# Moving the low-bits step of the w1 and w2 conversion from VectorE to ScalarE in a pooled-attention and gated-MLP kernel

## The chip, the cores and the metric

The kernel runs on one core of one Trainium2 chip. The core has five engines that each work through their own queue in order: TensorE (PE in the profile, with its weight loads as PEld), VectorE (DVE), ScalarE (ACT), GpSimd (POOL) and SyncE (SP), which here only issues DMAs. The metric is the device time of one execution in microseconds. Before the change the median of three runs is 786.11 us (785.08 to 788.28).

## The reference

Attention over 8 batches, 8 heads, 576 tokens and 64 dimensions, whose keys and values are averaged over groups of 8 tokens, and then an MLP over the 4608 tokens:

```python
k_p = k.reshape(B, H, 72, 8, D).mean(axis=3)
v_p = v.reshape(B, H, 72, 8, D).mean(axis=3)
attn = softmax(q @ k_p.T / sqrt(D))
x = (attn @ v_p) as (4608, 512)
a = x @ w1                  # w1, w2: 512 x 1024
b = x @ w2
h = a * b @ w3              # w3: 1024 x 1024
out = h @ w_out             # w_out: 1024 x 512, result float32
```

q, k and v are float32. The four weights are float64, so each of their values is two 32-bit words in memory, and the kernel itself makes float32 values of them.

## The kernel before, in words

**Weights.** The kernel multiplies w3 by w_out once, to a matrix W (`w_mm`, line 624), so that the MLP is (a * b) @ W. A float32 operand is split into a high part and a low part (`split`, lines 152 and 153: ScalarE copies to the reduced type, VectorE or GpSimd subtracts), and three matmuls stand for one product (`PASSES`).

**From float64 to float32.** A weight tile arrives as a raw cell: 128 partitions of 1024 int32 words, that is 512 float64 values. Three steps make float32 bits of it. `high` (line 135, ScalarE, Prelu) turns the high word into z. `low` (line 140, VectorE) shifts the low word right by 29, which leaves its top three bits in r. `conv_b` (line 148, VectorE) joins them as (z << 3) | r. `conv_a` is `high` and `low` together. For w1 and w2, `w12_conv` calls `conv_a` for one cell out of 16 (eight column groups j, two matrices w), `w12_conv2` calls `conv_b`, and `w12_split` splits the result into hl cells: its copy is on ScalarE, its subtraction on GpSimd, except for the three cells of LO_DVE. The results r lie in five buffers that are used in turn, z in three. The conversion of w3 and w_out uses the same helpers, in `w_block` and `w_conv`.

**Main loop.** The tokens go in 12 chunks m of 384. For each chunk and each of eight column groups j, TensorE computes a = x w1 (12 matmuls, line 563, tile a), b = x w2 (12 matmuls, line 563, tile b), and adds the product g = a * b times W to three accumulators (9 matmuls, line 598). ScalarE copies a (line 573), VectorE multiplies (line 583), ScalarE makes g's high part gh (line 584), VectorE its low part gl (line 589). The attention of chunk n is woven into the MLP of chunk n-1: scores (line 404), their minimum (line 420) and exponential (line 422, 425 and 426, or for some token tiles of the first two chunks line 430 on ScalarE alone), the scaling by the sum (lines 439 to 442), the remainder columns R (ScalarE line 451, VectorE line 453), the transposes of E and R on TensorE (lines 464 and 474) and their copies (lines 520 to 527), the product with v (lines 537 to 540) and its split into xT (lines 548 and 549). The pooled keys km are summed by VectorE (line 319) or GpSimd (lines 362 to 364) and turned by TensorE (line 328).

**What sets the order.** The order is written by hand. `at(kind, k, ...)` puts each piece at a step k; pieces are sorted by whole step, then loads, vector work (P), main matmuls (M) and attention matmuls (A), then by the fraction of the step. All engines run what they get in that order. With M0 = 36 the step at which the main loop begins, the conversion of cell i = 2j + w stands at step M0 - 6 + 1.25 i, its `conv_b` one step later and its split four steps later. So the sixteen conversions lie between the last products for W and the first chunk of the MLP.

PSUM tiles of the attention (`att`) rotate through three buffers: a transpose of R at line 474 can start only when the engines have read the score tile that held its buffer before.

Of the kernel before, what the change touches and what calls it, by code (L numbers as in the profile page):

```python
# [8 lines left out]
F32 = mybir.dt.float32  # L9
F32R = mybir.dt.float32r  # L10
I32 = mybir.dt.int32
AF = mybir.ActivationFunctionType
ALU = mybir.AluOpType
AX = mybir.AxisListType
# [4 lines left out]
def kernel(  # L19
# [14 lines left out]
    nc = tc.nc  # L34
# [41 lines left out]
        out=msk,  # L76
        in_=ident.rearrange("p (a two e) -> p two a e", two=2, e=2 * KR),
# [10 lines left out]
    def f(ap):  # L88
        return ap.bitcast(F32)
# [4 lines left out]
    def raw_cell(i):  # L94
        return cp.tile([P, 1024], I32, tag=f"c{i}", name="raw")

# [4 lines left out]
    def W_cell(s, i, dt):  # L101
        return cp.tile([P, DM], dt, tag=f"W{s}_{i}", name="Wc")

    raw, w3t, wo, w12, W = {}, {}, {}, {}, {}
    FREED = (8, 0, 9, 1, 10, 2, 11, 3, 12, 4, 13, 5, 14, 6, 15, 7)
    w1r, w2r, w3r, wor = (w.bitcast(I32) for w in (moe_w1, moe_w2, moe_w3, moe_w_out))
    stage = {}
# [22 lines left out]
    def high(c, z):  # L130

        w = c.rearrange("p (c t) -> p c t", t=2)
        nc.scalar.activation(out=z, in_=w[:, :, 1].bitcast(F32), func=AF.Prelu, scale=2.0 ** -112, alpha=2.0 ** 32)

    def low(c, r):

        w = c.rearrange("p (c t) -> p c t", t=2)
        nc.vector.tensor_scalar(out=r, in0=w[:, :, 0], scalar1=29, scalar2=None, op0=ALU.logical_shift_right)  # L140

    def conv_a(c, r, z):
        high(c, z)
        low(c, r)

    def conv_b(r, z):

        nc.vector.scalar_tensor_tensor(  # L148
            out=r, in0=z.bitcast(I32), scalar=3, in1=r, op0=ALU.logical_shift_left, op1=ALU.bitwise_or)

# [4 lines left out]
    def w_tiles(s):  # L155
        if s == 0:
            stage["wt"] = [t[:, i] for t, x in (
                (p1.tile([P, x, 512], I32, tag=tag, name="wt"), x)
                for tag, x in (("PTh", 3), ("PTx", 4))) for i in range(x)]
        if s < NJ:  # L160
            stage["wo", s] = stage["wt"][s % 4], f(stage["wt"][4 + s % 3])
        stage["w3", s] = W_cell(0, 4 + s % 4, I32), W_cell(1, 4 + s % 4, F32)

# [45 lines left out]
    def w_conv(s):  # L209
        w_tiles(s)  # L210
        conv_a(raw.pop(("w3", s)), *stage["w3", s])
# [9 lines left out]
    def w12_conv(j, w):  # L221
        i = 2 * j + w
        if i == 0:
            wb = [xp.tile([P, 3, 512], I32, tag=f"xT{x}", name="wb") for x in range(2)]
            spare = [osp.tile([P, 512], I32, tag="ob", name="wb") for _ in range(2)]
            stage["wb"] = [wb[0][:, x] for x in range(3)] + spare, [wb[1][:, x] for x in range(3)]
        r, z = stage["wb"]
        stage["w12", j, w] = r[i % 5], f(z[i % 3])
        conv_a(raw.pop(("w12", j, w)), *stage["w12", j, w])

    def w12_conv2(j, w):
        conv_b(*stage["w12", j, w])
# [144 lines left out]
    def prep_vr(b):  # L377
# [4 lines left out]

        nc.scalar.activation(out=f(hi), in_=f(hi), func=AF.Copy, scale=msk[:, 0:1])
        nc.scalar.activation(out=m, in_=m, func=AF.Copy, scale=msk[:, 1:2])
        stage["vrp", b] = f(hi), m
# [25 lines left out]
    def soft1(n, t, half):  # L411
# [9 lines left out]
        if (n, t) not in SOFT_ACT:  # L421
            nc.vector.tensor_tensor(  # L422
                out=E[:nt, hs], in0=sv,
                in1=mx[:nt, hs].unsqueeze(2).broadcast_to([nt, 4, KP]), op=ALU.subtract)
            nc.scalar.activation(out=E[:nt, hs], in_=E[:nt, hs], func=AF.Exp, scale=-1.0)  # L425
            nc.vector.reduce_sum(out=sm[:nt, hs], in_=E[:nt, hs], axis=AX.X)  # L426
            return
        for i in range(4):
            h = 4 * half + i
            nc.scalar.activation(  # L430
                out=E[:nt, h], in_=sv[:, i], func=AF.Exp, scale=-1.0, bias=mx[:nt, h:h + 1],
                accum_out=sm[:nt, h:h + 1])
# [290 lines left out]
    for j in range(NJ):  # L723
        for w in range(2):
            i = 2 * j + w
            at("L", K0 + 8.5 + i, load_w12, j, w)
            k = M0 - 6 + 1.25 * i
            at("P", k, w12_conv, j, w)
            at("P", k + 1, w12_conv2, j, w)
            at("P", k + 4, w12_split, j, w)  # L730
# [66 lines left out]
```

## Time and profile before

| | |
|---|---|
| median of three runs | 786.11 us (785.08 to 788.28) |
| profiled execution, its own time | 787.77 us |
| span of the profiled execution, first to last instruction | 785.9 us |
| granted TensorE clock, mean | 0.991 |
| busy: TensorE, weight loads, VectorE, ScalarE, GpSimd | 97%, 90%, 61%, 35%, 26% of the span |

How to read it: a group's row names line, engine, operation, the written and the read tile, the shape and the count; a duration is of the instruction itself, waiting for a port or an operand inside the instruction included. In a timeline row the first number is the start in us from the start of the span, the second the time it covers, and the bracket says how long the engine had been idle and who released it. In the answer for one source line, three numbers are the shortest, median and longest duration in ns.

### The profile page before, as it was taken

How to read it: one execution, taken by the hardware profiler on the slowest of the kernel's cores; microseconds unless marked ns; L12 is line 12 of the kernel's file. 1: busy time of each engine (PE TensorE's matmuls, PEld its weight loads, DVE VectorE, ACT ScalarE, POOL GpSimd, SP SyncE). 2: the span in 40 equal slices, each digit the busy share in tenths (PEclk: the TensorE clock that was granted, in tenths of full speed). 3: DMA queues.
4: the chain of work that ended last, by engine and by line, in shares of the span. 5: the costliest groups of instructions: out<-in, count | busy, mean ns of one | idle time of the engine just before them, and what ended most of it. 6: DMA issues, size and time to landing. Idle time of an engine off the chain costs nothing.

```text
span 785.9 us, 11514 instructions
## 1 busy us (share of the span) xinstructions
PE 759.7 (97%) x4146; PEld 703.7 (90%) x4146; DVE 479.2 (61%) x939; ACT 278.5 (35%) x694; POOL 201.1 (26%) x234
## 2 busy tenths in 40 slices
PE   8898888999999999999999999999999999999998
PEld 7677777899999998999999998999999998999997
DVE  6957988576475477476484586574574675662211
ACT  5566655332233233232233233332332333332211
POOL 2254564204307403005208202016125220000000
PEclk9999999999999999999999999999999999999999
DMA  9998970016326332036144223037144232120101
GB/s 328 292 209 200 282 152 10 1 61 129 66 79 134 71 98 55 16 86 140 32 129 93 77 81 71 15 101 140 41 122 94 75 75 47 47 55 1 40 1 41
DMA packets 123913, 74.43 MB, mean 95 GB/s; under 512 B 75600, under 2 KB 107600, under 8 KB 123856
## 3 DMA queue, kind: packets, MB, share of 16 engines
q1 hardware_dynamic: 123856, 73.69, 38.2%
q8 instruction: 33, 0.54, 0.3%
q14 instruction: 24, 0.20, 0.1%
HBM read 52.43 MB, written 9.44 MB: 79 GB/s over the span
## 4 chain that ended last, share of the span: by engine, by line
PE 74%; DVE 15%; ACT 3%; DMA 3%; issue 3%; SPq 1%; DVEq 0%
PE o L598 22%; PE a L563 21%; PE b L563 21%; PE att L404 3%; DMA st<-in_v_dram 2%; PE o L624 2%; DVE T L487 2%; DVE E L442 1%; DVE wb L148 1%; DVE wb L140 1%; PE att L538 1%; PE att L540 1%; PE att L539 1%; DVE mx L420 1%; PE att L537 1%
## 5 line engine op out<-in xcount | busy, mean ns | idle before, releaser
L563 PE MATMUL a<-xT,hl 128*128 128x384 f32 x1152 | 222.1, 341 | 0.0
L563 PE MATMUL b<-xT,hl 128*128 128x384 f32 x1152 | 220.8, 339 | 0.4 <-DVE Wc L153 0.4
L563 PEld LDWEIGHTS a<-xT,hl 128*128 128x128 f32 x1152 | 202.5, 189 | 4.5 <-POOL hl L153 0.2
L563 PEld LDWEIGHTS b<-xT,hl 128*128 128x128 f32 x1152 | 199.7, 188 | 0.8 <-DVE Wc L153 0.8
L598 PE MATMUL o<-Wc,gh 128*128 128x512 f32 x576 | 180.6, 395 | 0.0
L362 POOL TENSOR_TENSOR st<-st 72x512 f32<-72x512 f32 (+1 forms) x53 | 77.8, 1469 | 224.5 <-DMA st<-in_k_dram 172.1
L598 PEld LDWEIGHTS o<-Wc,gh 128*128 128x128 f32 x576 | 106.7, 188 | 17.0
L583 DVE TENSOR_TENSOR a<-b,a 128x384 f32<-128x384 f32 x96 | 52.8, 550 | 112.6 <-PE b L563 112.6
L598 PE MATMUL o<-Wc,gl 128*128 128x512 f32 x288 | 114.3, 397 | 3.1 <-DVE gl L589 3.1
L584 ACT CAST gh<-a 128x384 fp32r<-128x384 f32 x96 | 49.2, 513 | 154.8 <-DVE a L583 154.8
L573 ACT COPY a<-a 128x384 f32<-128x384 f32 x96 | 46.0, 479 | 109.8 <-PE a L563 88.0
L425 ACT ACTIVATE E<-E 128x288 f32<-128x288 f32 (+1 forms) x70 | 31.1, 445 | 123.4 <-DVE E L422 123.4
L589 DVE TENSOR_TENSOR gl<-a,gh 128x384 fp32r<-128x384 f32 x96 | 64.0, 667 | 13.0 <-ACT gh L584 13.0
L598 PEld LDWEIGHTS o<-Wc,gl 128*128 128x128 f32 x288 | 54.1, 188 | 16.9 <-DVE gl L589 4.4
L549 DVE TENSOR_TENSOR xT<-att,xT 128x384 fp32r<-128x384 f32 x48 | 26.5, 556 | 60.3 <-ACT xT L548 60.3
L375 POOL TENSOR_TENSOR vbd<-vm,vbd 64x256 fp32r<-64x256 f32 x16 | 12.1, 759 | 180.1 <-ACT vbd L374 179.5
L426 DVE TENSOR_REDUCE sm<-E 128x4 f32<-128x288 f32 (+1 forms) x70 | 31.6, 452 | 35.8 <-ACT E L425 35.8
L404 PE MATMUL att<-kbd,qT 128*128 128x144 f32 (+1 forms) x320 | 52.6, 288 | 0.2 <-ACT E L430 0.2
L404 PEld LDWEIGHTS att<-kbd,qT 128*128 128x128 f32 (+1 forms) x320 | 47.8, 180 | 4.3 <-ACT E L430 0.5
L153 DVE TENSOR_TENSOR PTx<-PTx,PTh 128x512 fp32r<-128x512 f32 (+1 forms) x33 | 24.7, 749 | 35.1 <-ACT PTh L152 31.7
L420 DVE TENSOR_REDUCE mx<-att 128x4 f32<-128x288 f32 (+1 forms) x80 | 35.3, 441 | 17.7 <-PE att L404 17.6
L363 POOL TENSOR_TENSOR st<-st 72x256 f32<-72x256 f32 (+1 forms) x53 | 44.4, 837 | 4.2
(91 smaller groups left out, 811.6 us busy)
## 6 DMA issues: line engine op xcount, KB each, us to landing
raw<-in_moe_w_dram SPq DMA_DIRECT2D x32, 512.0 KB
PTx<-T SPq DMA_DIRECT2D x120, 96.0 KB
st<-in_k_dram SPq DMA_DIRECT2D x32, 288.0 KB
out_dram<-ob SPq DMA_DIRECT2D x35, 256.0 KB
st<-in_v_dram SPq DMA_DIRECT2D x32, 256.0 KB
qs<-in_q_dram SPq DMA_DIRECT2D x128, 48.0 KB
raw<-in_moe_w_out_dram SPq DMA_DIRECT2D x8, 512.0 KB
st<-in_v_dram SPq DMA_DIRECT2D x64, 64.0 KB
```

What stands on the lines that cost most here:

```text
L362: nc.gpsimd.tensor_tensor(out=t[:, :, 0:4], in0=t[:, :, 0:4], in1=t[:, :, 4:8], op=ALU.add)
L363: nc.gpsimd.tensor_tensor(out=t[:, :, 0:2], in0=t[:, :, 0:2], in1=t[:, :, 2:4], op=ALU.add)
L404: nc.tensor.matmul(out=ps[:nt, 2 * KP * j:2 * KP * (j + 1)], lhsT=qT[n][:, pr, off:off + nt], rhs=kbd[b % 2][:, pr], start=True, stop=True,)
L420: nc.vector.tensor_reduce(out=mx[:nt, hs], in_=sv, axis=AX.X, op=ALU.min)
L425: nc.scalar.activation(out=E[:nt, hs], in_=E[:nt, hs], func=AF.Exp, scale=-1.0)
L426: nc.vector.reduce_sum(out=sm[:nt, hs], in_=E[:nt, hs], axis=AX.X)
L563: nc.tensor.matmul(out=o, lhsT=w12[j, w][sw][:, kt * P:(kt + 1) * P], rhs=x[sx][:, kt], start=(i == 0), stop=(i == 3 * NK - 1))
L573: nc.scalar.copy(out=a, in_=gt[m, j][:, :CH])
L583: nc.vector.tensor_tensor(out=g, in0=ps[:, :CH], in1=g, op=ALU.mult)
L584: nc.scalar.copy(out=gh, in_=g)
L589: nc.vector.tensor_tensor(out=gl, in0=g, in1=f(gh), op=ALU.subtract)
L598: nc.tensor.matmul(out=oacc[m][t], lhsT=(gh, gl)[sg][:, c], rhs=W[j][sw], start=(j == 0 and i == 0), stop=(j == NJ - 1 and i == 2))
```

## The change

`w12_conv` hands `conv_a` another function for the low bits, `low_act`. It reads the raw cell as uint16, four halves to a float64 value, and takes the second of them, the upper half of the low word. ScalarE computes half * 2^-13 + 2^-14 - 0.5, and the conversion to int32 at the write rounds to the nearest whole number, which is the half shifted right by 13: the same three bits as the low word shifted right by 29. VectorE's shift (line 140) is no longer issued for w1 and w2; for w3 and w_out it stays.

```diff
+U16 = mybir.dt.uint16
...
+    def low_act(c, r):
+
+        w = c.bitcast(U16).rearrange("p (c t) -> p c t", t=4)
+        nc.scalar.activation(out=r, in_=w[:, :, 1], func=AF.Copy, scale=2.0 ** -13, bias=2.0 ** -14 - 0.5)
+
-    def conv_a(c, r, z):
+    def conv_a(c, r, z, low=low):
         high(c, z)
         low(c, r)
...
-        conv_a(raw.pop(("w12", j, w)), *stage["w12", j, w])
+        conv_a(raw.pop(("w12", j, w)), *stage["w12", j, w], low=low_act)
```

## The prediction

> **What bounds the kernel now.** I read the page's first two parts, then the waits of TensorE between 65 and 160 us, then the timelines of VectorE, ScalarE, GpSimd and TensorE in that stretch, and the answers for the two source lines that are exchanged.
>
> ```profile
> PE 759.7 (97%) x4146; PEld 703.7 (90%) x4146; DVE 479.2 (61%) x939; ACT 278.5 (35%) x694; POOL 201.1 (26%) x234
> ...
> PE   8898888999999999999999999999999999999998
> ...
> DVE  6957988576475477476484586574574675662211
> ```
>
> A slice is 19.6 us. From the eighth slice on TensorE is at 9 almost to the end, so what is gained or lost before about 142 us moves all that follows, one for one. VectorE is fullest (7 to 9) in slices 4 to 7, which is where the sixteen conversions of w1 and w2 lie. TensorE's waits there, in order of their totals (us in total, times, longest):
>
> ```profile
> PE att L474 <- ACT E L430: 4.8, 2, 3.9
> PE att L474 <- DVE E L422: 2.0, 1, 2.0
> PE att L328 <- DVE km L319: 1.6, 1, 1.6
> ...
> PE b L563 <- DVE Wc L153: 0.4, 1, 0.4
> ```
>
> The four rows are 8.8 us together: this is the purse from which a gain can come. All of them end on chains through VectorE and ScalarE.
>
> ```profile
> L140 DVE TENSOR_SCALAR wb<-raw x16: 410/550/1528, 73.0 to 129.8; 128x512 int32<-128x512 int32 x16
> ...
> L140 DVE TENSOR_SCALAR wb<-raw 128x512 int32<-128x512 int32 x16 | 12.8, 802 | 0.0
> ...
> L135 ACT ACTIVATE wb<-raw x16: 652/670/718, 72.3 to 127.6; 128x512 f32<-128x512 f32 x16
> ...
> L135 ACT ACT_TABLE_LOAD  x1: 1283/1283/1283, 0.7 to 0.7; - x1
> ```
>
> The sixteen shifts take 12.8 us of VectorE, 802 ns on average, though the shortest takes 410 ns.
>
> **The change part by part.** Removed: sixteen shifts on VectorE. Added: sixteen ScalarE instructions over 512 elements a partition, each directly behind its `high`. No row of this trace has ScalarE reading 16-bit values or writing int32. The nearest is `high` itself (L135): the same count, the same engine, the same 8-byte step between elements, 652 to 718 ns. The rows below show that the next ScalarE instruction starts 0.55 to 0.57 us after it (87.68 to 88.23, 112.81 to 113.38), so I charge p = 0.57 us; as bounds I take 0.47 below (0.1 less) and 0.72 above (the longest L135 with no overlap). For the price alone, the Trainium skill, page "ScalarE: Activation LUTs", section "What ACT_TABLE_LOAD costs", gives 186 ns + 0.833 ns an element for immediate scale and bias and an overlap of 93 ns: an estimate of 0.52 us, by which the gain worked out below would be 4.9 us instead of 4.6.
>
> No DMA moves, and SP's and POOL's queues keep their order. Reading a raw cell now involves ScalarE alone. The new instruction waits for its r buffer, last read by a subtraction five cells back; behind it on ScalarE would queue the copies of the split and of the MLP. That wait should be over:
>
> ```profile
> 101.81 1.65 POOL L153 TENSOR_TENSOR hl<-wb,hl 128x512 fp32r<-128x512 f32 x1 [2.80 <-ACT hl L152]
> ...
> 105.08 0.66 ACT L135 ACTIVATE wb<-raw 128x512 f32<-128x512 f32 x1
> ```
>
> Cell 10's buffer is free at 103.46, and ScalarE would want it at 105.65; both move earlier alike. I charge nothing; if that cover were gone, the 2.2 us would turn to a wait of ScalarE.
>
> Now along the path. *Before 96.5 us:*
>
> ```profile
> 87.68 0.65 ACT L135 ACTIVATE wb<-raw 128x512 f32<-128x512 f32 x1
> 88.23 0.58 ACT L152 CAST Wc<-b 128x512 fp32r<-128x512 f32 x1
> ...
> 88.84 0.69 DVE L153 TENSOR_TENSOR Wc<-b,Wc 128x512 fp32r<-128x512 f32 x1 [1.00 <-ACT Wc L152]
> ...
> 92.63 1.51 DVE L140 TENSOR_SCALAR wb<-raw 128x512 int32<-128x512 int32 x1
> 94.06 0.55 DVE L583 TENSOR_TENSOR a<-b,a 128x384 f32<-128x384 f32 x1
> 94.53 1.92 DVE L319 TENSOR_REDUCE km<-st 72x128 f32<-72x1024 f32 x1
> ...
> 96.51 0.28 PE L328 MATMUL att<-ident,km 72*128 72x72 f32 x1 [1.58 <-DVE km L319]
> ```
>
> The sixth new instruction lands between the L135 at 87.68 and the cast of W at 88.23, for which VectorE has already waited 1.00 us and on which the first b matmul depends: everything is p = 0.57 us later. Then the shift at 92.63 goes, whose successor started 1.43 us later (I count each shift so: its duration less 0.07 to 0.08 of overlap). The next instruction, L583, reads PSUM and keeps its 0.55 us. So km, and with it L328 after its wait of 1.58, comes 1.43 - 0.57 = 0.86 us earlier.
>
> *To the wait at 112.97:*
>
> ```profile
> 97.44 0.42 DVE L140 TENSOR_SCALAR wb<-raw 128x512 int32<-128x512 int32 x1
> 97.96 1.60 DVE L148 SCALAR_TENSOR_TENSOR wb<-wb 128x512 int32<-128x512 int32 x1
> 99.48 0.41 DVE L140 TENSOR_SCALAR wb<-raw 128x512 int32<-128x512 int32 x1
> ...
> 104.50 0.41 DVE L140 TENSOR_SCALAR wb<-raw 128x512 int32<-128x512 int32 x1
> ...
> 108.93 1.48 DVE L140 TENSOR_SCALAR wb<-raw 128x512 int32<-128x512 int32 x1
> ...
> 111.13 0.44 DVE L420 TENSOR_REDUCE mx<-att 96x4 f32<-96x288 f32 x1
> ...
> 112.97 0.58 PE L474 MATMUL att<-ident,R 96*128 96x96 f32 x2 [3.86 <-ACT E L430]
> 113.26 3.71 PE L563 MATMUL a<-xT,hl 128*128 128x384 f32 x12
> ```
>
> Four shifts stand between km and the minimum at 111.13: 0.35 + 0.34 + 0.34 + 1.41 = 2.44 us. The minimum and the exponential behind it come 0.86 + 2.44 = 3.30 us earlier; TensorE's wait of 3.86 shrinks to 1.4. ScalarE has gaps here, so the new instructions hide in them. The twelve matmuls at 113.26 took 3.71 us, against 2.33 us after the shorter wait of 1.96 (rows at 133.80 and 133.94 below): that slow stretch should go too, but TensorE then only waits longer at the next place, so I count nothing for it.
>
> *To 123.42:*
>
> ```profile
> 112.81 0.68 ACT L135 ACTIVATE wb<-raw 128x512 f32<-128x512 f32 x1
> 113.38 0.62 ACT L152 CAST hl<-wb 128x512 fp32r<-128x512 f32 x1
> ...
> 114.44 1.33 DVE L589 TENSOR_TENSOR gl<-a,gh 128x384 fp32r<-128x384 f32 x1 [0.87 <-ACT gh L584]
> ...
> 117.39 0.95 DVE L140 TENSOR_SCALAR wb<-raw 128x512 int32<-128x512 int32 x1
> ```
>
> VectorE waits for gh, and a new instruction goes in ahead of gh: 0.57 us lost. (The shift ahead of that wait gains nothing.) The shift at 117.39 gives back 0.87. The next minimum is 3.30 - 0.57 + 0.87 = 3.60 us earlier.
>
> *To 133.80:*
>
> ```profile
> 123.25 0.67 ACT L135 ACTIVATE wb<-raw 128x512 f32<-128x512 f32 x1
> ...
> 129.03 0.43 ACT L451 CAST R<-E 96x64 fp32r<-96x64 f32 x2
> ...
> 124.56 1.53 DVE L140 TENSOR_SCALAR wb<-raw 128x512 int32<-128x512 int32 x1
> ...
> 129.76 1.38 DVE L140 TENSOR_SCALAR wb<-raw 128x512 int32<-128x512 int32 x1
> ...
> 132.20 0.60 DVE L453 TENSOR_TENSOR R<-E,R 96x64 fp32r<-96x64 f32 x2
> ...
> 133.80 0.35 PE L474 MATMUL att<-ident,R 96*128 96x96 f32 x2 [1.96 <-DVE E L422]
> 133.94 2.33 PE L563 MATMUL a<-xT,hl 128*128 128x384 f32 x12
> ```
>
> From 123.25 to 129.46 ScalarE has no gap, and three new instructions go in: 1.71 us. Its R copy, which ended 132.20 - 129.46 = 2.74 us before VectorE took it, now decides: 3.60 - 1.71 + 2.74 = 4.63 us earlier at L453. On VectorE's side alone it would be 3.60 - 0.57 + 1.45 + 1.30 = 5.78, so ScalarE is the later one. The minimum behind it releases L474 at 133.80. After it no shift is left, and TensorE is full from 142 us.
>
> The sum is a gain of 4.6 us: 787.77 becomes 783.1 for the profiled execution. That execution lies 1.7 us above the median of 786.11, so against the median the forecast is 781.5. With p the sum reads 7.48 - 5 p: 5.1 us at 0.47, 3.9 at 0.72, nothing at 1.50.
>
> **The rivals.** *The stall is inherited.*
>
> ```profile
> 107.76 2.37 POOL L362 TENSOR_TENSOR st<-st 128x512 f32<-128x512 f32 x1
> ```
>
> The shift at 108.93 took 1.48 us where 0.41 would do, and GpSimd was at work from 107.76 to 110.13, until 0.3 us before the shift ended. The neighbours wait in the same way: L148 at 97.96 takes 1.60. If the instruction behind the shift only takes its wait over, a shift is worth 0.34. The one at 92.63 keeps its worth (L583 follows). Then the terms are 0.86 + 1.37 = 2.23, 2.23 - 0.57 + 0.34 = 2.00, and on VectorE 2.00 - 0.57 + 0.34 + 0.34 = 2.11: 784.0 us. For it speaks that an L453, an L589 or an L153 of VectorE follows, all reading two SBUF tiles; against it that GpSimd's instruction will stand elsewhere. The Trainium skill, page "SBUF — State Buffer", section "Who interferes with whom", has this as its rule: VectorE and GpSimd share a port pair, whoever issues first holds it for its whole instruction, and a VectorE instruction with two SBUF inputs is blocked as well. By that rule the shorter sum holds; the trace agrees as far as the 410 and 1528 ns of one instruction go.
>
> *The waits of others melt too.* A join (L148) needs the shift's result; between the shift's end at 97.86 and the join at 97.96 lies a gap of 0.1 us in which GpSimd can get in ahead. Without the shift the join at 97.96 might take no longer than L153 at 88.84, 0.69 instead of 1.60; with one more such join that is some 2 us more, 779.5.
>
> *ScalarE is slower than its row.* Any p from 0.72 to 1.50 gives 782.2 to 786.
>
> *Slower than before.* If the Copy with an integer write needed a table of its own, each would cost one load of 1.28 us there and one back, p = 0.57 + 2.57 = 3.14, and 7.48 - 15.7 is a loss of 8.2 us: 794.3. It decides from p = 1.50. Against it: one load in the whole run serves Prelu, Exp and Copy.
>
> That the change doesn't do what it says comes to the same as the last two: the new instruction would be more than one.
>
> **How the numbers follow.** A measurement of this kernel can tell about 0.5% from no change, 3.9 us: faster is below 782.2, slower above 790.0. The forecast has 0.51, with a range of its own of 779.5 to 783; the melting waits 0.12; the inherited stall 0.25; a slower ScalarE 0.06; the table loads 0.06. Of the forecast's 0.51 I put 0.09 above 782.2. Faster: 0.42 + 0.12 = 0.54. Same: 0.09 + 0.25 + 0.06 = 0.40. Slower: 0.06. The range runs from 778.5 (under the melting waits' 779.5) to 786.5 (over the inherited stall and a slower ScalarE) and leaves out the table loads and the tails.
>
> **What would show it.** Right: sixteen ScalarE instructions `wb<-raw` of 0.6 to 0.7 us writing int32; L140 with 24 left; the b matmul's wait on L153 up from 0.4 to about 1.0 us; the wait of 3.9 at the first L474 down to about 1.4, and the matmuls behind it at 2.3 instead of 3.7; L474 before 133.80 now released later than VectorE alone would allow, with VectorE idle on ScalarE's R. Wrong: L453, L589 or L153 longer by what the shift lost (inherited stall); a second ACT_TABLE_LOAD, or a new instruction over 1 us; a wait of ScalarE on GpSimd's L153 for r.

## The result, and the profile after

The changed kernel takes 782.78 us (median of 20 runs, 779.69 to 786.02), the kernel before 787.96 us (20 runs, 783.82 to 791.66): a ratio of 0.9933, 95% interval 0.9918 to 0.9948. That is 5.2 us faster; the forecast was 4.6 us, to 781.5 from a median of 786.11. The profiled execution took 784.37 us, with a span of 782.6.

The top of its page (busy time, then the slices of TensorE, VectorE and ScalarE):

```profile
PE 758.2 (97%) x4146; PEld 701.9 (90%) x4146; DVE 466.9 (60%) x923; ACT 287.1 (37%) x710; POOL 198.7 (25%) x234
...
PE   7898998999999999999999999999999999999998
...
DVE  5967887576475486484474585574564675662211
ACT  4666876332233233232332333222232332332211
```

VectorE has 16 instructions fewer and ScalarE 16 more. The same shift of work shows in the stage itself. The sums of busy time from 70 to 140 us, kernel before and then changed kernel:

```profile
sum 70.00, PE 60.74 PEld 53.95 DVE 64.53 ACT 43.37 POOL 41.13; mean PE 15.19 PEld 13.49 DVE 16.13 ACT 10.84 POOL 10.28
```

```profile
sum 70.00, PE 63.34 PEld 55.65 DVE 55.76 ACT 55.76 POOL 41.12; mean PE 15.84 PEld 13.91 DVE 13.94 ACT 13.94 POOL 10.28
```

VectorE was busy 64.5 of 70 us. Now VectorE and ScalarE are busy equally long, 55.8 us each. (These profiles show times and types, not values: that the integers which ScalarE writes are those of the shift, no run here shows.)

What was added and what remains (the answers for line 146, the new instruction, and the groups of line 136, `high`, and 154, the join, between 65 and 145 us):

```profile
L146 ACT ACTIVATE wb<-raw x16: 642/668/702, 74.7 to 126.3; 128x512 int32<-128x512 uint16 x16
```

```profile
L136 ACT ACTIVATE wb<-raw 128x512 f32<-128x512 f32 x16 | 10.8, 678 | 0.0
L146 ACT ACTIVATE wb<-raw 128x512 int32<-128x512 uint16 x16 | 10.7, 672 | 0.0
```

```profile
L154 DVE SCALAR_TENSOR_TENSOR wb<-wb 128x512 int32<-128x512 int32 x16 | 15.7, 983 | 2.4 <-ACT wb L146 2.4
```

The new instruction costs what `high` costs, and the sixteen joins wait 2.4 us for it in all. TensorE's waits between 65 and 160 us in the changed kernel:

```profile
PE att L480 <- DVE R L459: 2.8, 2, 2.6
PE att L410 <- ACT E L436: 1.5, 2, 0.7
PE att L480 <- ACT E L436: 1.5, 1, 1.5
PE b L569 <- DVE Wc L159: 1.0, 1, 1.0
PE att L480 <- DVE E L428: 0.9, 1, 0.9
PE att L470 <- DVE E L448: 0.7, 1, 0.7
PE att L301 <- DVE xT L555: 0.5, 1, 0.5
PE att L334 <- DVE km L325: 0.3, 1, 0.3
```

The longest (2.6) lies before the stage. The wait of 3.9 us is gone, and the score matmuls (line 410) now wait 1.5 us for ScalarE's exponential, where it was 0.2. The places that the prediction names, in TensorE's timeline (line 212 is line 206 of before, the transposes just ahead of the first new instruction, and serves as a common mark):

```profile
73.16 0.60 PE L212 MATMUL att<-ident,Wc 128*128 128x128 f32 x4
...
91.61 2.37 PE L569 MATMUL b<-xT,hl 128*128 128x384 f32 x12 [0.98 <-DVE Wc L159]
...
97.18 0.28 PE L334 MATMUL att<-ident,km 72*128 72x72 f32 x1 [0.26 <-DVE km L325]
...
109.89 0.39 PE L480 MATMUL att<-ident,R 96*128 96x96 f32 x2
110.06 2.34 PE L569 MATMUL a<-xT,hl 128*128 128x384 f32 x12
113.15 0.73 PE L410 MATMUL att<-kbd,qT 128*96 128x144 f32 x4 [0.75 <-ACT E L436]
...
120.39 0.39 PE L480 MATMUL att<-ident,R 96*128 96x96 f32 x2 [1.48 <-ACT E L436]
...
130.24 0.36 PE L480 MATMUL att<-ident,R 96*128 96x96 f32 x2 [0.87 <-DVE E L428]
...
138.44 2.35 PE L569 MATMUL a<-xT,hl 128*128 128x384 f32 x12
```

In the kernel before, the first and the last of these rows read:

```profile
71.78 0.60 PE L206 MATMUL att<-ident,Wc 128*128 128x128 f32 x4
...
142.00 2.33 PE L563 MATMUL a<-xT,hl 128*128 128x384 f32 x12
```

I call the time between them the stage: 142.00 - 71.78 = 70.22 us before, 138.44 - 73.16 = 65.28 us after, 4.94 us less. The mark itself lies 1.38 us later than before, ahead of anything that was changed. A likely part of this is TensorE's clock, which was granted at 0.50 in some stretches (from 14.0 to 17.0 us in the kernel before) that fall differently in the two profiles: between 10 and 20 us the mean granted clock was 0.66 in this one and 0.83 in the one of before. How large that part is, is not shown. After the stage, from the last row above to the end of the span, both take the same: 785.9 - 142.0 = 643.9 and 782.6 - 138.4 = 644.2. Nothing was given back later.

### The profile page after: what moved, and what is told of

Its sections match the earlier page's. It is cut to its first block, busy times and chain, and to the rows that moved or that the text cites. A ratio compares the mean times of both kernels' runs of the same rounds, so it can differ in the third digit from the quotient of the medians.

```text
span 782.6 us, 11496 instructions
## 1 busy us (share of the span) xinstructions
PE 758.2 (97%) x4146; PEld 701.9 (90%) x4146; DVE 466.9 (60%) x923; ACT 287.1 (37%) x710; POOL 198.7 (25%) x234
## 4 chain that ended last, share of the span: by engine, by line
PE 77%; DVE 12%; ACT 5%; DMA 2%; issue 2%; SPq 1%; DVEq 0%
PE o L604 22%; PE b L569 21%; PE a L569 21%; PE att L410 4%; PE o L630 3%; DVE T L493 1%; ACT E L436 1%; DMA st<-in_v_dram 1%; PE att L544 1%; PE att L546 1%; PE att L545 1%; PE att L543 1%; DVE E L448 1%; DMA raw<-in_moe_w_out_dram 1%; DVE mx L426 1%
## 5 line engine op out<-in xcount | busy, mean ns | idle before, releaser
L368 POOL TENSOR_TENSOR st<-st 72x512 f32<-72x512 f32 (+1 forms) x53 | 75.2, 1420 | 224.8 <-DMA st<-in_k_dram 174.1
L630 PE MATMUL o<-hl 128*128 128x512 f32 x144 | 43.0, 436 | 3.1 <-DVE hl L183 3.1
```

What stands on the lines that cost most here:

```text
L368: nc.gpsimd.tensor_tensor(out=t[:, :, 0:4], in0=t[:, :, 0:4], in1=t[:, :, 4:8], op=ALU.add)
L630: nc.tensor.matmul(out=wacc[h][it], lhsT=w3t[s][sa][:, it * P:(it + 1) * P], rhs=wo[j][sb], start=(j == 0 and i == 0), stop=(j == NJ - 1 a ...
```

## The experiments

Ratios are to the kernel before, in runs on the same chip. "Stage" is the time between the two marks in the profiled execution.

| kernel | ratio (95% interval) | stage, us |
|---|---|---|
| before | 1 | 70.22 |
| changed; once more | 0.9933 (0.9918 to 0.9948); 0.9922 (0.9893 to 0.9950) | 65.28; 65.36 |
| 1 ScalarE's instruction added, shift kept | 0.9994 (0.9973 to 1.0015) | 70.09 |
| 2 no low bits | 0.9895 (0.9869 to 0.9921) | 64.12 |
| 3 ScalarE's instruction twice | 1.0034 (1.0014 to 1.0054) | 74.97 |
| 4 three cells kept on VectorE; once more | 0.9924 (0.9902 to 0.9947); 0.9905 (0.9875 to 0.9936) | 63.78; 63.98 |
| 5 five cells moved | 0.9958 (0.9934 to 0.9982) | 68.33 |
| 6 before, no GpSimd subtraction | 0.9875 (0.9846 to 0.9905) | 61.81 |
| 7 changed, no GpSimd subtraction | 0.9887 (0.9861 to 0.9913) | 61.80 |
| 8 changed, low bits and join later | 0.9924 (0.9897 to 0.9951) | 64.46 |
| 9 before, one-port form for the shift | 0.9966 (0.9944 to 0.9988) | 69.24 |
| 12 three kept and the rest later | 0.9892 (0.9864 to 0.9921) | 64.33 |

The stage came out within 0.2 us for the two kernels profiled twice, far closer than the runs agree. It holds only between kernels that reach the first mark at about the same time: number 5 reached it 3.7 us earlier than before, and TensorE then waited 1.64 us for xT (at 81.38), where before it did not wait. Numbers 6 and 7 reached it 3.2 us apart.

**1. ScalarE's cost alone.**

```diff
-        conv_a(raw.pop(("w12", j, w)), *stage["w12", j, w], low=low_act)
+        low_act(c, zz.bitcast(I32))
+        high(c, zz)
+        low(c, rr)
```

> VectorE keeps its shift, and ScalarE does the same work once more for nothing: it writes the low bits to z just before high overwrites z. So ScalarE's cost stands alone. Path theory (the instruction costs 0.57 us wherever ScalarE is what the chain waits for, and VectorE's relief is the whole gain): three of the new instructions lie on the path (the 6th, 12th and 14th cell), 1.7 us slower than before, about +0.2%. Rival, ScalarE hides it all: no difference, 0.0%. Rival, inherited stall (a shift is worth only its bare 0.34 us): says the same as the path theory here.

Measured: 0.9994, and a stage 0.13 us shorter. The added instructions cost nothing that can be measured; the 1.7 us of the path's sum lie outside the interval, which ends at +1.2 us. In the trace the b matmul is later, 19.21 us from the mark instead of 17.81, but the fourth group of a matmuls (line 563 before) is earlier, 40.53 instead of 41.48. The sum is wrong in taking each delay of ScalarE for a delay of all that follows. How the delay is won back is not shown.

**2. VectorE's relief alone.** The join takes a zero instead of r.

```diff
-        conv_a(raw.pop(("w12", j, w)), *stage["w12", j, w], low=low_act)
+        high(raw.pop(("w12", j, w)), stage["w12", j, w][1])
...
-        conv_b(*stage["w12", j, w])
+        nc.vector.scalar_tensor_tensor(
+            out=r, in0=z.bitcast(I32), scalar=3, in1=zero_r.broadcast_to([P, 512]),
+            op0=ALU.logical_shift_left, op1=ALU.bitwise_or)
```

> Leaves out the low three bits of the w1 and w2 values: no shift on VectorE, no instruction on ScalarE, and the join takes a constant zero instead, with two SBUF inputs as before. So VectorE's relief stands alone. Path theory: the sum with p = 0, 7.5 us faster than before (-0.95%), 2.9 us better than the changed kernel. Inherited stall: 0.34 us a shift save for the one at 92.63, 3.8 us faster (-0.5%). ScalarE hides it all: no better than the changed kernel, 5.2 us faster (-0.66%).

Measured: 0.9895, 8.3 us faster. The path's 7.5 lies in the interval (6.2 to 10.3 us); the 3.8 of the inherited stall and the 5.2 of a free ScalarE don't. So in the changed kernel ScalarE's instruction does cost something, though it costs nothing where the shift is still there. How much depends on the measure: about 3 us by the runs (0.9895 against 0.9933, with intervals that just overlap), 1.2 us by the stage (64.12 against 65.28 and 65.36). The stage is 6.1 us shorter than before, less than the path's 7.5.

**3. ScalarE's instruction twice.**

```diff
+        high(c, zz)
+        low_act(c, rr)
+        low_act(c, rr)
```

> The changed kernel with ScalarE's low-bits instruction issued twice, the second over the first. Path theory: 7.48 - 5 x 1.14 = 1.8 us faster than before (-0.2%). Inherited stall: 0.2 us faster, nothing to be seen. ScalarE hides it all: 5.2 us faster, as the changed kernel.

Measured: 1.0034, 2.7 us slower than before; all three theories are off. The second instruction costs 1.0034 - 0.9933 = 1.0%, 8 us (9.7 in the stage), where the path's sum has 2.9. In the sums from 70 to 140 us ScalarE is the fuller of the two by 14 us:

```profile
sum 70.00, PE 57.41 PEld 49.24 DVE 46.00 ACT 60.49 POOL 34.60; mean PE 14.35 PEld 12.31 DVE 11.50 ACT 15.12 POOL 8.65
```

And waits come that the sum did not have. Two of the longest of TensorE's between 60 and 160 us, and ScalarE and GpSimd in their timelines:

```profile
PE att L414 <- ACT E L440: 2.9, 2, 1.5
PE b L573 <- POOL hl L159: 2.1, 1, 2.1
```

```profile
102.84 1.38 ACT L146 ACTIVATE wb<-raw 128x512 int32<-128x512 uint16 x2 [1.05 <-POOL hl L159]
```

```profile
98.50 5.54 POOL L159 TENSOR_TENSOR hl<-wb,hl 128x512 fp32r<-128x512 f32 x2 [1.43 <-ACT hl L158]
```

ScalarE waits for a buffer r that GpSimd still reads (the cover that the prediction named), GpSimd had waited for ScalarE's copy, and TensorE waits for GpSimd's low part. In these runs the price of sixteen ScalarE instructions goes up from kernel to kernel: nothing that can be measured beside VectorE's shifts (number 1), 1 to 3 us without them (number 2 to the changed kernel), 8 to 10 us for the next sixteen.

**4 and its repeat. Three cells stay on VectorE.**

```diff
-        conv_a(..., low=low_act)
+        conv_a(..., low=low if i in (5, 11, 13) else low_act)
```

> The changed kernel, but the 6th, 12th and 14th cell (i = 5, 11, 13) keep VectorE's shift: before the change these three shifts ran while VectorE would have waited for ScalarE anyway, and their ScalarE instructions are the ones on the path. Path theory: 6.3 us faster than before (-0.8%), 1.7 us better than the changed kernel. Inherited stall: 3.8 us faster (-0.5%). ScalarE hides it all: 5.2 us or a little less, no better than the changed kernel.

> The version that keeps VectorE's shift for the 6th, 12th and 14th cell once more, beside the changed kernel on the same chip. Path theory: 1.7 us better than the changed kernel (0.2%). Rival: the same.

> The changed kernel once more, as the measure for the runs beside it: 5.2 us faster than before (-0.66%) by its first measurement, 4.6 us by the path's terms.

Measured: 0.9924 and 0.9905, against 0.9933 and 0.9922 for the changed kernel. Both times the lower of the pair, by 0.1 and 0.2%, but by less than the intervals can tell. The stage shows it: 63.78 and 63.98 against 65.28 and 65.36, 1.5 and 1.4 us shorter, where the path said 1.7. The two places at which the prediction booked a loss of 0.57 in TensorE's timeline of number 4:

```profile
92.09 2.37 PE L569 MATMUL b<-xT,hl 128*128 128x384 f32 x12 [0.44 <-DVE Wc L159]
...
120.66 0.39 PE L480 MATMUL att<-ident,R 96*128 96x96 f32 x2 [1.11 <-ACT E L436]
```

The wait of the b matmul is back at 0.44, from 0.98, and the second L480 waits 0.4 us less.

**5. Five cells moved**, those with the longest shifts.

```diff
+        conv_a(..., low=low_act if i in (6, 10, 12, 14, 15) else low)
```

> Only five cells (i = 6, 10, 12, 14, 15) have ScalarE's instruction, those whose VectorE shifts took 0.95 to 1.53 us before; the other eleven keep VectorE's shift. Path theory: 1.43 + 1.41 + 0.87 - 1.14 + 2.74 = 5.3 us faster than before (-0.67%), as much as moving all sixteen. Inherited stall: 2.8 us faster (-0.35%). Rival, load: the gain goes with the VectorE time taken away, 6.85 of 12.8 us, so 2.8 us faster.

Measured: 0.9958, 3.3 us (1.4 to 5.2). The path's 5.3 is just outside, the two rivals' 2.8 inside. The shifts kept in the first cells, which the sum gave no weight because no wait of TensorE lay behind them in the one trace it was made from, can count when TensorE arrives earlier: ahead of the wait for xT in this profile one of them (at 76.79) took 1.52 us. That this is the whole difference is not shown.

**6 and 7. GpSimd out of the way**: both kernels without the thirteen subtractions.

```diff
-        split(f(r), *w12[j, w], eng=nc.vector if (j, w) in LO_DVE else nc.gpsimd)
+        if (j, w) in LO_DVE:
+            w12[j, w] = hi, lo
+            split(f(r), hi, lo)
+        else:
+            w12[j, w] = hi, hi
+            nc.scalar.copy(out=hi, in_=f(r))
```

> The kernel before, without GpSimd's thirteen subtractions for w1 and w2: their low pass multiplies the high part a second time (the low parts are left out). GpSimd's pooling sums stay. Contention theory (long VectorE instructions are waits for GpSimd): VectorE's shifts fall from 802 ns on average to 600 or less, and the kernel is 2 to 5 us faster than before. Rival, GpSimd has no part in it: shifts stay at 0.8 us and the time is within 1 us.

> The changed kernel, without the same thirteen GpSimd subtractions. To be set against the run before it. Contention theory: with GpSimd out of the way a shift is worth less, so the change gains 2 to 3.5 us between these two instead of 5.2. Rival, GpSimd has no part: 5 us between the two as without the cut.

Measured: 0.9875 and 0.9887. Without GpSimd's subtractions the kernel before is 9.9 us faster, where at most 5 were expected, and the change gains nothing that can be seen, where 2 to 3.5 were expected: 0.1% the other way. The two intervals together rule out the 5 us of the rival, but not a gain of some 2 us. The groups of the shift and the join in number 6:

```profile
L148 DVE SCALAR_TENSOR_TENSOR wb<-wb 128x512 int32<-128x512 int32 x16 | 12.7, 791 | 1.1 <-ACT wb L135 0.8
L140 DVE TENSOR_SCALAR wb<-raw 128x512 int32<-128x512 int32 x16 | 9.1, 569 | 0.0
```

The shift falls from 802 to 569 ns on average, the join from 1015 to 791, with the same work. At the fourth group of a matmuls number 7 is still ahead, 36.35 us from the mark against 37.62; at the fifth 45.99 against 46.83; at the sixth and seventh they are level (55.00 and 55.03, 61.80 and 61.81). So what VectorE gains from the bare shifts, some 1.3 us, is lost again, for the most part while TensorE waits for ScalarE's exponential (2.1 us in number 7 from the fourth group on, 1.1 in number 6).

The pair has a rival that it does not exclude. TensorE and the r buffers wait for the subtractions too, and with these gone the waits of TensorE in the stage add up to 4.1 us instead of 10.1. So there is less left for any change to shorten, whether or not the shifts collide.

**8. Low bits and join 0.8 steps later.**

```diff
...
+            at("P", k + 0.8, w12_low, j, w)
-            at("P", k + 1, w12_conv2, j, w)
+            at("P", k + 1.8, w12_conv2, j, w)
```

> The changed kernel with ScalarE's low-bits instruction 0.8 steps later than high, behind the casts of W, behind gh and behind the exponentials of the second half tile, and the join 0.8 steps later too. Path theory: the losses at the 6th and 12th cell go, the three instructions ahead of the last R copy stay: 5.8 us faster than before (-0.73%), 1.1 us better than the changed kernel. Rival, ScalarE's load alone counts: the same as the changed kernel (-0.66%). Should the late join be what the splits wait for, it is worse than the changed kernel.

Measured: 0.9924, and a stage of 64.46, 0.8 and 0.9 us under the changed kernel's two, where the path said 1.1. The direction is the path's; the runs can't tell the kernels apart.

**9. A VectorE instruction that doesn't share the port.** In the kernel before, the shift is replaced.

```diff
...
+        nc.vector.tensor_scalar(
+            out=f(rr), in0=c.bitcast(mybir.dt.uint16).rearrange("p (c t) -> p c t", t=4)[:, :, 1],
+            scalar1=0.0, scalar2=None, op0=ALU.mult, op1=ALU.add, accum_out=sums)
```

> The kernel before, but VectorE's shift is replaced by another VectorE instruction over the same 512 elements that also sums them up, a form that runs at one element a cycle and, by the Trainium skill, page SBUF - State Buffer, section Who interferes with whom, does not take the port pair that it shares with GpSimd. It multiplies by zero, so the low three bits are left out. An estimate from 288 elements in 0.44 us (line 420): about 0.7 us each with the reading of the sum, against 0.34 bare and 0.73 on average for the shift. Collision theory: every one takes the same time, VectorE's excess over the shortest duration of each instruction falls from 19.9 by about 6 us, and by the path's terms with 0.7 for each the kernel is 1.9 us faster than before (-0.25%). Inherited stall: the collisions only move to the neighbours, each instruction costs 0.35 us more than the bare shift, and the kernel is 3 us or more slower (+0.4%).

The answer for its line:

```profile
L234 DVE TENSOR_SCALAR_CACHE_REDUCE wb<-raw x16: 667/672/679, 73.1 to 129.3; 128x512 f32<-128x512 uint16 x16
L234 DVE DVE_READ_ACCUMULATOR wb<-raw x16: 73/76/81, 73.7 to 129.9; 128x1 f32 x16
```

667 to 679 ns, whatever GpSimd does, where the shift took 410 to 1528. The kernel is 2.7 us faster than before (0.9966, 0.9944 to 0.9988; 1.0 us in the stage) although each instruction is longer than a bare shift. That is what the collision theory said (1.9), and the opposite of the inherited stall (3 slower). Some of the stall does move on: the joins' time over their shortest (worked out as in the next section) goes from 5.6 to 7.1 us. The trace agrees here with the Trainium skill, page "SBUF — State Buffer", section "Who interferes with whom", which says that the accumulating form of this instruction doesn't take the shared pair. The run changes the type and the arithmetic along with the form, so it does not tell which of them matters.

**12. Three kept and the rest later.**

```diff
+        if i in (5, 11, 13):
+            low(...)
...
+        if 2 * j + w not in (5, 11, 13):
+            low_act(...)
```

> The three cells kept on VectorE and ScalarE's instruction of the other thirteen 0.8 steps later, with the join 0.8 steps later for all. Path theory: only the 15th and 16th cell's instructions are left ahead of the last R copy, as with the three kept alone: 6.3 us faster than before (-0.8%), the later join brings nothing more. Rival: the two gains add up to more, 7 us or over (-0.9%).

Measured: 0.9892, 8.5 us faster than before and the lowest of all versions that leave nothing out. It beats the kernel before clearly. Its median is 2.1 us under the changed kernel's beside it (780.81 and 782.87) and its stage 1.0 us (64.33 and 65.36), but the intervals overlap, and the stage isn't shorter than number 4's. That it beats the changed kernel is likely, not shown.

## Why the prediction was right

Right in sign and size: 5.2 us against 4.6, and 4.94 in the stage. That the two agree so closely is in part luck: up to the minimum the sum is 1.15 us short, and behind it 0.84 too long (it books 1.33 more, measured are 0.49). Point by point, all measured from the mark, changed kernel less kernel before:

| place | predicted | measured |
|---|---|---|
| first b matmul | +0.57 | +0.64 |
| L328, behind km | -0.86 | -0.71 |
| minimum ahead of the first R transpose | -3.30 | -4.45 |
| second L474 (123.42) | -3.60 | -4.41 |
| third L474 (133.80) | -4.63 | -4.94 |

*The price of the new instruction.* Predicted 652 to 718 ns from L135; measured 642 to 702. The new instruction starts 0.55 to 0.59 us behind `high`.

*The first two places* came as said, with a wait of 0.98 us for the cast of W in place of 0.4.

*The minimum* came 1.15 us earlier than the sum. Here the rival of the melting waits was partly true. VectorE's timeline of the changed kernel:

```profile
97.65 0.55 DVE L595 TENSOR_TENSOR gl<-a,gh 128x384 fp32r<-128x384 f32 x1
98.12 0.68 DVE L154 SCALAR_TENSOR_TENSOR wb<-wb 128x512 int32<-128x512 int32 x1
98.72 0.45 DVE L426 TENSOR_REDUCE mx<-att 96x4 f32<-96x288 f32 x1
...
104.99 1.78 DVE L154 SCALAR_TENSOR_TENSOR wb<-wb 128x512 int32<-128x512 int32 x1
106.95 1.18 DVE L459 TENSOR_TENSOR R<-E,R 96x64 fp32r<-96x64 f32 x2 [0.18 <-ACT R L457]
108.06 0.44 DVE L426 TENSOR_REDUCE mx<-att 96x4 f32<-96x288 f32 x1
```

The join that took 1.60 us at 97.96 takes 0.68 at 98.12, as that rival said. Another, at 104.99, has a collision of its own now (1.78). So single joins inherit a stall and others lose theirs. To see the balance I took from each VectorE instruction of the stage the shortest duration that the same operation on the same tiles and shapes has in any of these runs, and summed what was over: 19.95 us before, 6.33 of it in the shifts; 12.93 after. The others' share went from 13.63 to 12.93: in total the stall was not inherited.

*The wait of 3.86 us* was forecast to shrink to 1.4; it is gone. The twelve matmuls behind it take 2.34 us instead of 3.71, as forecast.

*The last part.* ScalarE was to decide ahead of the third L474, through its R copy. VectorE's timeline shows ScalarE deciding, but through the split's copy two instructions earlier:

```profile
127.50 0.93 DVE L159 TENSOR_TENSOR hl<-wb,hl 128x512 fp32r<-128x512 f32 x1 [1.30 <-ACT hl L158]
128.35 0.89 DVE L459 TENSOR_TENSOR R<-E,R 96x64 fp32r<-96x64 f32 x2
```

*What the prediction had not seen:* two waits of 0.7 us of the score matmuls (line 410) on ScalarE's exponential, behind a ScalarE that now has the new instructions ahead of it.

*What was right for a reason that held less than stated.* By the runs the sum 7.48 - 5 p is a fair line through p = 0 (8.3 us measured) and p = 0.57 (5.2). By the stage it isn't: 6.1 and 4.9 us, so the five prices of 0.57 us that the sum adds up cost 1.2 us instead of 2.9. At twice the price it fails by either measure: it says 1.8 faster and the chip 2.7 slower.

*What the gain is.* The sum counted shifts by their durations, and the trace of the kernel before shows what those durations contain. The eight shifts of 681 ns and more each began beside a GpSimd instruction and ended 0.28 to 0.29 us behind its end. Two of these instructions are subtractions, as here, six GpSimd's other work, as at 107.76 in the prediction:

```profile
124.51 1.29 POOL L153 TENSOR_TENSOR hl<-wb,hl 128x512 fp32r<-128x512 f32 x1 [5.85 <-ACT hl L152]
```

```profile
124.56 1.53 DVE L140 TENSOR_SCALAR wb<-raw 128x512 int32<-128x512 int32 x1
```

The five shifts with no GpSimd instruction beside them took 411 to 414 ns. The other three took 410 to 419; one of them, at 97.44, ran beside a GpSimd subtraction that itself took 2.70 us, where the shortest took 1.28. So the long shifts wait for GpSimd, and of the 12.8 us of all sixteen 6.3 are such waits. Number 9 agrees: an instruction that doesn't wait makes the kernel faster though it is longer than the bare shift. That these waits are the whole of the gain is not shown; the pair 6 and 7 would fit, but leaves the rival named there.

*Left open:* whether and by how much number 12 beats the changed kernel, why five cells gave less than the path's sum, and why the price of the new instruction differs between runs and stage.

## What to carry to other kernels

Before an instruction is moved off an engine, compare its longest with its shortest duration, and look at what the other engines do while the long ones last: here half of the shifts' time was waiting, not work. Watch how full the receiving engine becomes in the stage that counts: with VectorE and ScalarE at 55.8 us each, sixteen more ScalarE instructions cost 8 us by the runs, where the first sixteen cost 1 to 3. Where an engine would be waiting anyway, the instruction may as well stay (number 4, by the stage). And when a change is worth less than run medians scatter, look at the stage between two marks, but only between kernels that reach the first mark at about the same time.

## What the runs showed of the hardware

ScalarE reads 16-bit halves at an 8-byte step and writes int32 in the time of a float32 pass: 668 and, for line 135 before the change, 670 ns at the median over 512 elements. VectorE's accumulating form takes 667 to 679 ns over 512 elements beside a busy GpSimd, the plain shift 410 to 1528. The eight shifts that took 681 ns or more all ended 0.28 to 0.29 us behind the end of a GpSimd instruction beside which they began. And the stretches in which TensorE's clock was granted at 0.50 in the first 70 us are not the same in two executions, whose same point of the program lay 1.4 us apart, a quarter of what the change is worth.
